# Four edits to the start of a three-layer kernel: more warming matmuls, two weight loads moved in the queue, two more large tiles, one split issued later

## The chip, the cores and the metric

The kernel runs on one core of a Trainium2 chip. The metric is the device time of one execution in microseconds. The kernel before has a median of 984.3 us over three runs (981.82 to 985.46). The execution that was profiled took 988.99 us; its span in the trace, from the first to the last instruction, is 987.2 us.

## The reference

The input x has 2 batches of 3008 rows of 256 numbers. Three layers follow one another:

```python
X = np.fft.fft(np.fft.fft(x, axis=1), axis=2).real        # (2, 3008, 256)
t = X.reshape(6016, 256)
h = t @ w_in;   t = (h / (1 + exp(-h))) @ w_out            # 256 -> 2048 -> 256
h = t @ w2_in;  t = (max(h, 0) + alpha * min(h, 0)) @ w2_out   # 256 -> 2048 -> 256
```

The weights arrive as 64-bit floats, so each one is converted to 32 bits on the chip.

## The kernel before, in words

**The transform** is a 64 by 47 factorisation of the 3008 rows, followed by the transform along the 256 columns. For each batch b it has three stages. Stage A (`stage_a`, L248) folds symmetric parts of x on DVE and POOL and multiplies by a 128x128 matrix that lies in `cs`; batch 0 uses the matrix as it is, batch 1 uses it split into a high and a low part, `fh` and `fl` (the split is a copy on ACT and a subtraction on DVE, L165 and L166). Its result `ya` goes to DRAM as `ys` and comes back transposed as `y`. Both ways are cut into three parts (`K_PARTS`): `store` (L295) writes part k, `load_y` (L312) reads it, with two stores and four loads for each part. Stage B (`stage_b`, matmul L325) multiplies y into `z`, in five groups for each half h; the first two groups need part 0 of y, the next two part 1, the last one part 2. Stage C (`stage_c`, matmul L355) makes `eo` and `n` from z, in three chunks of 502 columns for each batch.

**The first expert layer** has 96 iterations (six chunks of columns, 16 blocks of 128 of the 2048 hidden units). An iteration has six matmuls into `pe` and `po` (L560 to L562), three steps on DVE (`t`, `hp`, `t`: L568, L571, L572), Silu on ACT (`gh`, L575, and again L576), two subtractions `gl` (L588) on POOL or DVE, and twelve matmuls into accumulators (L608 to L612), two iterations later. The first 16 iterations run over blocks 0 to 7 of chunks 0 and 1. Weights come in four groups g of four blocks each: `load_w1(g)` issues two DMAs of 512 KB, `load_o1(g)` one of 1024 KB (both through `load_raw`, L393). A conversion is one ACT step (L181) and four DVE steps (L185 to L197) for each 512 columns; the high and low parts follow (L432, L435, L450, L454). Group 1 is used from iteration 4 on.

**The second expert layer** has the same sizes and runs afterwards, with its order written out by hand. Its coefficients come from `alpha` by six small POOL steps (`coefficients`, L483 to L488).

**What sets the order.** The start, up to stage C of the first chunk, stands in a `manual_schedule` block: each engine issues its instructions in the order of the text. All DMAs are issued by SP, one after another, and a DMA that waits holds up those behind it. Part 0 of y is stored and loaded first; 12 fp32 matmuls `warm` (L783, two records in the trace for each) follow stage A on PE. After stage C's first chunk the text stores part 1 of ys, loads part 1 of y, loads group 1's w_in, alpha, stores part 2, loads group 1's w_out and loads part 2 of y. Behind this block a planner, with its own costs of instructions, orders the rest up to the second expert layer. `put` gives each step the iteration in which it stands in the program's text (`PLAN`), and the planner may issue it earlier where an engine has nothing to do. `behind` forbids a step to be issued before a named instruction.

**Large tiles.** The pool `big` has 10 buffers of 8 KB in each partition. Pieces of x, raw weights, `ya`, `y`, `z` and `eo` take them in turn, so a load has to wait until the last user of its buffer is done.

Of the kernel before, what the change touches and what calls it, by code (L numbers as in the profile page):

```python
# [25 lines left out]
PLAN = {  # L26
# [5 lines left out]
}  # L32
# [15 lines left out]
F_PARTS = (0, 8, 16)  # L48
ORDER = [(c, f) for f0, f1 in zip(F_PARTS, F_PARTS[1:]) for c in range(2) for f in range(f0, f1)]
ORDER += [(c, f) for c in range(2, NC) for f in range(NF)]  # L50
WARM = 12
WARM0 = 8
SUM0 = "vpapap"
I1_AT = 0
# [11 lines left out]
FA0, FR0, R0, RS0, CD0, SD0, SG0, OD0, NCONST = 0, 128, 256, 444, 634, 762, 890, 1018, 1146  # L66
# [53 lines left out]
def fft_moe_kernel(  # L120
# [12 lines left out]
    nc = tc.nc  # L133
    wp = ctx.enter_context(tc.tile_pool(name="wp", bufs=1))
    dp = ctx.enter_context(tc.tile_pool(name="dp", bufs=1, space=bass.MemoryType.DRAM))
    bp = ctx.enter_context(tc.tile_pool(name="bp", bufs=10))
    ep = ctx.enter_context(tc.tile_pool(name="ep", bufs=3))
    cp = ctx.enter_context(tc.tile_pool(name="cp", bufs=5))
    kp = ctx.enter_context(tc.tile_pool(name="kp", bufs=16))
# [4 lines left out]
    def big(shape, dt, name):  # L144
        return bp.tile(shape, dt, tag="big", name=name)
# [4 lines left out]
    def conv(dt, name):  # L150
        return cp.tile([128, 512], dt, tag="cv", name=name)

    def mm_ps(name, w=512):
        return pm.tile([128, w], F32, tag="mm", name=name)
# [9 lines left out]
    def split(hi, lo, src, lo_eng=None):  # L164
        nc.scalar.activation(hi, src, AF.Copy)  # L165
        return (lo_eng or nc.vector).tensor_tensor(lo, src, hi.bitcast(F32), op=ALU.subtract)  # L166
# [57 lines left out]
    cs = wp.tile([128, CD0], F32, tag="cs", name="cs")  # L224
    fh = wp.tile([128, 128], F32R, name="fh")
    fl = wp.tile([128, 128], F32R, name="fl")
# [13 lines left out]
    def load_x(b, i, parts):  # L240
        n0, n1 = PIECES[i : i + 2]
        X[b, i] = t = big([128, 512 * (n1 - n0)], F32, f"x{b}_{i}")
        w = 512 * (n1 - n0) // parts
        for j in range(parts):
            at = 512 * n0 + j * w
            nc.sync.dma_start(t[:, j * w : (j + 1) * w], xs[b, :, at : at + w])
# [142 lines left out]
    def load_raw(key, *srcs):  # L389
        RAW[key] = t = big([128, 1024, 2], U32, f"raw_{key}")  # L390
        w = 2048 // len(srcs)
        for i, src in enumerate(srcs):
            nc.sync.dma_start(  # L393
                t.rearrange("p n t -> p (n t)")[:, i * w : i * w + w], src.bitcast(U32)
            )

    def load_half(key, src, i, at=None):
        if key not in RAW:
            RAW[key] = big([128, 1024, 2], U32, f"raw_{key}")
        at = i * 512 if at is None else at  # L400
        t = RAW[key].rearrange("p n t -> p (n t)")
        return nc.sync.dma_start(t[:, i * 1024 : i * 1024 + 1024], src[:, at : at + 512].bitcast(U32))
# [9 lines left out]
    def load_w1(g):  # L412
        load_raw(f"i{g}", wi1[0, :, 512 * g : 512 * g + 512], wi1[1, :, 512 * g : 512 * g + 512])

    def load_o1(g):
        load_raw(f"o{g}", wo1[:, 1024 * g : 1024 * g + 1024])

    def prep_w1(g):
        v = {}
        t = []  # L420

        def total(eng):
            wi_tiles(1, g)
            t.append(conv(F32, f"we{g}"))
            eng.tensor_tensor(t[0], v[0][0], v[1][0], op=ALU.add)

        def rest(eng):
            eng.tensor_tensor(v[0][0], v[0][0], v[1][0], op=ALU.subtract)
            t.append(v[0][0])

        def high(j):
            nc.scalar.activation(WI[1, g, 2 * j], t[j], AF.Copy)  # L432

        def low(j, eng):
            eng.tensor_tensor(WI[1, g, 2 * j + 1], t[j], WI[1, g, 2 * j].bitcast(F32), op=ALU.subtract)  # L435

        post = [either(total), either(rest)]
        for j in range(2):
            post += [lambda j=j: high(j), either(lambda eng, j=j: low(j, eng))]
        v[0], st0 = to_f32(None, (f"i{g}", 0, 512), f"i{g}_0")  # L440
        v[1], st1 = to_f32(None, (f"i{g}", 512, 512), f"i{g}_1")
        return [(st0, []), (st1, post)]
# [331 lines left out]
    def run(steps):  # L774
        for s in steps:
            (s if callable(s) else s[0])()

    def warm(w, x, n):
        if n == 0:
            return  # L780
        ps = mm_ps("warm")
        for j in range(n):
            nc.tensor.matmul(ps[:, : x.shape[1]], w, x, start=True, stop=True)  # L783

    if True:
        with tc.manual_schedule():
            zero = conv(F32, "zero")
            nc.vector.memset(zero[:, :256], 0.0)
            warm(zero[:, :128], zero[:, :256], WARM0)
            nc.vector.memset(sm, 0.0)  # L790
            nc.scalar.activation(sm[:1, :1], sm[:1, :1], AF.Silu)
            for j in range(len(PIECES) - 1):
                load_x(0, j, (PIECES[j + 1] - PIECES[j]) // 2)
                if j == 0:
                    nc.sync.dma_start(cs[:, :R0], cst[:, :R0])
            cc = conv(F32, "cc")
            for g in range(2):
                load_half("i0", wi1[g], g, 0)
                if g == 0:
                    nc.sync.dma_start(cc, cst[:, CD0:])  # L800
                    nc.sync.dma_start(w128_raw.rearrange("p n t -> p (n t)"), w128.bitcast(U32))
            nc.sync.dma_start(cs[:, R0:], cst[:, R0:CD0])
            fold, mm, rest = stage_a(0)
            (i00, _), (i01, after_i0) = prep_w1(0)
            for (h, i), n in zip(A_ORDER, A_WARM):
                if h == 0:
                    fold(i)
                mm(h, i)
                warm(cs[:, FA0 : FA0 + 128], cs[:, :256], n)
            load_half("o0", wo1, 0)  # L810
            for h in range(2):
                load_y(0, h, 0)
            load_half("o0", wo1, 1)
            warm(cs[:, FA0 : FA0 + 128], cs[:, :256], WARM)
            (s0, p0), (s1, p1) = prep_o1(0)
            w128_st = to_f32(lambda: w128_sb, ("w128", 0, NF), "w128")[1]
            run(i00[:4])
            run(i01[:2])
            run(w128_st[:1])
            nc.scalar.activation(ch, cc, AF.Copy)  # L820
            run(i00[4:])
            for ab in zip(i01[2:], w128_st[1:]):
                run(ab)
            run(w128_st[4:])
            nc.vector.tensor_tensor(cl, cc[:, : SG0 - CD0], ch.bitcast(F32)[:, : SG0 - CD0], op=ALU.subtract)
            for n, (st, pool) in enumerate(zip(after_i0, SUM0)):
                (st if callable(st) else st[pool == "v"])()
                if n == 2:
                    run(s0)
            b00, b01 = stage_b(0, 0), stage_b(0, 1)  # L830
            run(b00[:2])
            run(b01[:2])
            run(p0)
            run(s1[:EARLY_O0])
            run(stage_c(0, 0))
            rest(1)
            for h in range(2):
                load_y(0, h, 1)
            load_w1(1)
            nc.sync.dma_start(alpha_sb, alpha)  # L840
            rest(2)
            load_o1(1)
            for h in range(2):
                load_y(0, h, 2)
        n1 = NC * NF
# [9 lines left out]
        def put(a, b, steps):  # L855

            for j, st in enumerate(steps):
                plan.setdefault(a + (b - a) * j // len(steps), []).append(st)
# [5 lines left out]
        def behind(st, *at):  # L864
            with ExitStack() as stack:
                for k in at:
                    stack.enter_context(tc.issue_after(LAST[k].ins))
                run([st])
# [4 lines left out]
                nc.gpsimd.tensor_copy(cx[64 * j : 64 * j + 1, :], ch[:1, OD0 - CD0 : OD0 - CD0 + 128])  # L873

        put(*PLAN["cx"], [mixed_cosines])
        put(*PLAN["fa"], [lambda: split(fh, fl, cs[:, FA0 : FA0 + 128])])
        put(*PLAN["o0"], [lambda st=st: behind(st, 0, ("low", 0)) for st in s1[EARLY_O0:] + p1])
        put(*PLAN["i1"], [lambda st=st: behind(st, 0, ("t", I1_AT)) for st in staged(prep_w1(1))])
        put(*PLAN["o1"], staged(prep_o1(1)))
# [129 lines left out]
```

## Time and profile before

| | |
|---|---|
| median of three runs | 984.3 us |
| profiled execution / its span | 988.99 us / 987.2 us |
| PE busy | 957.9 us, 97% of the span |
| DVE busy | 780.8 us, 79% |
| ACT busy | 710.7 us, 72% |
| POOL busy | 405.4 us, 41% |
| data moved by DMA | 37.05 MB, all issued by SP |

A busy engine is one that executes an instruction. A start time in the trace is counted from the start of the span. In the rows "x14" means 14 instructions merged into one row, and what stands in brackets is the idle time of the engine before the row and what ended it. "PEclk" is the granted clock of TensorE, where 1.00 is 2.4 GHz and 0.50 is 1.2 GHz.

### The profile page before, as it was taken

What the parts mean: (1) busy time and instruction counts of PE and PEld (TensorE: products, weight loads), DVE (VectorE), ACT (ScalarE), POOL (GpSimd) and SP (SyncE); (2) the same over time, 40 slices, a digit from 0 to 9 for tenths busy, and PEclk for the clock granted to TensorE, in tenths of its full rate; (3) what the DMA queues carried; (4) which work ended last, traced back from release to release, by engine and by line L of the source; (5) the groups of instructions that cost most, each with busy time, mean ns of one, the idle gap of its engine ahead of it and who ended that gap; (6) DMA issues with size and microseconds to landing.
All of it is one profiled execution on the core that took longest, in us unless ns stands there. A gap on an engine that the chain in (4) does not pass through costs nothing.

```text
span 987.2 us, 14338 instructions
## 1 busy us (share of the span) xinstructions
PE 957.9 (97%) x5170; PEld 824.7 (84%) x5170; DVE 780.8 (79%) x1328; ACT 710.7 (72%) x1410; POOL 405.4 (41%) x355
## 2 busy tenths in 40 slices
PE   7889899999999999999899999999999999999998
PEld 5768787888878788787789999999999999999997
DVE  6888898676796876958687887878878788787876
ACT  3557566665667666666887888878888788787875
POOL 2677869333257467697641221312213122131200
PEclk9789999999999999999999999999999999999999
DMA  8730300230110201100000000000000000000000
GB/s 264 235 122 3 105 22 1 52 104 1 43 43 9 94 1 43 43 9 35 1 1 22 1 22 22 1 21 1 21 9 14 21 1 21 2 22 21 1 21 21
DMA packets 16614, 37.05 MB, mean 38 GB/s; under 512 B 1824, under 2 KB 11296, under 8 KB 14880
## 3 DMA queue, kind: packets, MB, share of 16 engines
q1 hardware_dynamic: 16544, 36.15, 11.1%
q8 instruction: 40, 0.66, 0.3%
q14 instruction: 30, 0.25, 0.1%
HBM read 26.83 MB, written 9.31 MB: 37 GB/s over the span
## 4 chain that ended last, share of the span: by engine, by line
PE 78%; DVE 9%; issue 5%; POOL 4%; ACT 3%; DMA 1%; SPq 0%; POOLq 0%; ACTq 0%; DVEq 0%
PE a L768 27%; PE ac L670 20%; PE a L610 5%; PE a L612 5%; PE a L608 5%; PE b L670 3%; POOL gl L588 2%; PE po L560 1%; PE po L561 1%; PE pe L560 1%; PE po L562 1%; DVE hp L571 1%; PE pe L562 1%; PE pe L561 1%; PE psb L325 1%
## 5 line engine op out<-in xcount | busy, mean ns | idle before, releaser
L768 PE MATMUL a<-gh,wo 128*128 128x502 f32 x768 | 268.2, 391 | 0.0
L588 POOL TENSOR_TENSOR gl<-t,gh 128x502 fp32r<-128x502 f32 x96 | 131.6, 1371 | 95.1 <-ACT t L576 81.6
L768 PEld LDWEIGHTS a<-gh,wo 128*128 128x128 f32 x768 | 145.0, 189 | 23.2
L737 DVE SCALAR_TENSOR_TENSOR h<-h,fc,q 128x502 f32<-128x502 f32 x192 | 130.3, 679 | 38.4 <-ACT q L732 35.7
L610 PE MATMUL a<-gl,wo 128*128 128x502 f32 x384 | 148.3, 395 | 4.1 <-POOL gl L588 4.1
L768 PE MATMUL a<-gl,wo 128*128 128x502 f32 x384 | 149.7, 391 | 0.0
L612 PE MATMUL a<-gh,wo 128*128 128x502 f32 x384 | 147.3, 393 | 0.0
L748 DVE TENSOR_TENSOR gl<-h,gh 128x502 fp32r<-128x502 f32 x192 | 140.5, 732 | 0.1
L575 ACT ACTIVATE gh<-hp 128x502 fp32r<-128x502 f32 x96 | 59.7, 622 | 92.6 <-DVE hp L571 90.6
L608 PE MATMUL a<-gh,wo 128*128 128x502 f32 x384 | 122.8, 397 | 1.2 <-ACT gh L575 0.8
L743 ACT ACTIVATE gh<-h 128x502 fp32r<-128x502 f32 x192 | 118.5, 617 | 2.1 <-DVE h L737 2.1
L732 ACT ACTIVATE q<-h,fc 128x502 f32<-128x502 f32 x192 | 116.9, 609 | 3.0 <-DVE h L715 1.5
L646 POOL TENSOR_TENSOR xt<-o 128x252 f32<-128x252 f32 x24 | 16.7, 716 | 187.2 <-ACT q L732 131.1
L568 DVE SCALAR_TENSOR_TENSOR t<-n,sm,pe 128x502 f32<-128x502 f32 x96 | 70.2, 731 | 29.0 <-PE pe L562 25.3
L610 PEld LDWEIGHTS a<-gl,wo 128*128 128x128 f32 x384 | 73.2, 191 | 20.7 <-POOL gl L588 5.9
L588 POOL TENSOR_TENSOR gl<-hp,gh 128x502 fp32r<-128x502 f32 x52 | 69.4, 1335 | 47.6 <-ACT hp L576 39.8
L571 DVE TENSOR_TENSOR hp<-t,po 128x502 f32<-128x502 f32 x96 | 64.5, 672 | 29.5 <-PE po L562 23.8
L608 PEld LDWEIGHTS a<-gh,wo 128*128 128x128 f32 x384 | 72.2, 191 | 17.5 <-ACT gh L575 2.2
L612 PEld LDWEIGHTS a<-gh,wo 128*128 128x128 f32 x384 | 73.1, 190 | 15.0
L768 PEld LDWEIGHTS a<-gl,wo 128*128 128x128 f32 x384 | 72.5, 189 | 7.7
L704 ACT ACTIVATE u<-ac 128x252 f32<-128x252 f32 x96 | 36.6, 381 | 51.6 <-PE ac L670 51.6
L656 POOL TENSOR_TENSOR os<-o,os 128x252 fp32r<-128x252 f32 x36 | 32.5, 918 | 94.5 <-ACT os L655 92.6
(191 smaller groups left out, 2296.0 us busy)
## 6 DMA issues: line engine op xcount, KB each, us to landing
out_t<-ot SPq DMA_DIRECT2D x24, 251.0 KB, 2.5
x<-in_xs SPq DMA_DIRECT2D x8, 512.0 KB, 5.6
raw_i<-in_wi SPq DMA_DIRECT2D x8, 512.0 KB, 4.7
raw_w<-in_wi SPq DMA_DIRECT2D x4, 1024.0 KB, 5.0
raw_w<-in_wo SPq DMA_DIRECT2D x4, 1024.0 KB, 4.8
raw_o<-in_wo SPq DMA_DIRECT2D x3, 1024.0 KB, 5.6
y<-ys SPq DMA_DIRECT2D x16, 144.0 KB, 2.9
x<-in_xs SPq DMA_DIRECT2D x2, 1024.0 KB, 4.8
```

Source lines behind the costliest of these rows:

```text
L568: nc.vector.scalar_tensor_tensor(t, E128[c], w128_sb[:, f : f + 1], pe, op0=ALU.mult, op1=ALU.add)
L571: nc.vector.tensor_tensor(hp, t, po, op=ALU.add)
L588: (nc.gpsimd if s or lo_pool(i + 1) else nc.vector).tensor_tensor(lo, h, hi.bitcast(F32), op=ALU.subtract)
L608: nc.tensor.matmul(ACC1[lb, s], hi, G[i, s][0], start=st, stop=False)
L610: nc.tensor.matmul(ACC1[lb, s], hi, G[i, s][1], start=False, stop=False)
L612: nc.tensor.matmul(ACC1[lb, s], lo, G[i, s][0], start=False, stop=sp)
L670: nc.tensor.matmul(to, w, x, start=start and q == 0, stop=q == 2, skip_group_check=True)
L732: nc.scalar.activation(h["q", i][:, to], source(n, part), AF.Abs, scale=coef(n, i, 1))
L737: nc.vector.scalar_tensor_tensor(h[f"h{i}"][:, to], source(n, part), coef(n, i, 0), h["q", i][:, to], op0=ALU.mult, op1=ALU.add)
L743: nc.scalar.activation(hi, H[n][f"h{i}"], AF.Copy)
L748: nc.vector.tensor_tensor(lo, H[n][f"h{i}"], G[n, i][0].bitcast(F32), op=ALU.subtract)
L768: nc.tensor.matmul(ACC2[lb], w[lb][j], x, start=st and first, stop=sp and last)
```

## The change

`WARM` goes from 12 to 20: eight more matmuls (16 records) behind stage A. `load_w1(1)` and `load_o1(1)` move ahead, from behind the loads of y's part 1 to the place right behind the second half of group 0's w_out; all three DMAs now stand ahead of the stores of ys parts 1 and 2. The pool of large tiles has 12 buffers, and the scratch for dynamic DMAs is set to 1024 bytes. The split of stage A's matrix for batch 1 is put `behind` the last instruction of stage C's first chunk.

```diff
-WARM = 12
+WARM = 20
...
-    bp = ctx.enter_context(tc.tile_pool(name="bp", bufs=10))
+    bp = ctx.enter_context(tc.tile_pool(name="bp", bufs=12))
...
             load_half("o0", wo1, 1)
+            load_w1(1)
+            load_o1(1)
             warm(cs[:, FA0 : FA0 + 128], cs[:, :256], WARM)
...
             for h in range(2):
                 load_y(0, h, 1)
-            load_w1(1)
             nc.sync.dma_start(alpha_sb, alpha)
             rest(2)
-            load_o1(1)
             for h in range(2):
                 load_y(0, h, 2)
...
-        put(*PLAN["fa"], [lambda: split(fh, fl, cs[:, FA0 : FA0 + 128])])
+        put(*PLAN["fa"], [lambda: behind(lambda: split(fh, fl, cs[:, FA0 : FA0 + 128]), 0)])
...
-    nc = _bacc.Bacc("TRN2", target_bir_lowering=False, num_devices=1)
+    nc = _bacc.Bacc("TRN2", target_bir_lowering=False, num_devices=1, dynamic_dma_scratch_size=1024)
```

## Rows read from the trace of the kernel before

**Rows 1.** The page's slices: granted clock in 40 slices of 24.7 us, in tenths.
```profile
PEclk9789999999999999999999999999999999999999
```

**Rows 2.** Stretches: start:end, length, busy us (count) by engine, clock, DMA share, GB/s.
```profile
8.60:16.20 7.60, 7.13 (x25) 4.17 (x25) 6.03 (x12) 3.73 (x8) 2.61 (x5) 1.00 0.91 351
16.20:21.60 5.40, 5.40 (x27) 4.43 (x25) 4.12 (x10) 2.30 (x6) 0.00 (x0) 1.00 0.76 165
21.60:25.00 3.40, 0.00 (x1) 0.03 (x1) 2.08 (x7) 1.79 (x3) 2.50 (x4) 0.97 0.83 250
25.00:35.00 10.00, 10.00 (x37) 8.80 (x38) 6.41 (x13) 4.03 (x11) 4.85 (x4) 0.50 0.74 219
35.00:57.00 22.00, 16.44 (x78) 12.53 (x77) 21.90 (x33) 13.41 (x27) 17.68 (x18) 0.97 0.67 226
57.00:62.00 5.00, 5.00 (x13) 3.96 (x13) 2.76 (x6) 2.97 (x5) 5.00 (x4) 0.50 0.25 101
```

**Rows 3.** Timeline of PE: start us, length us, engine, line, operation, tiles, shapes, count.
```profile
16.18 5.43 PE L783 MATMUL warm<-cs 128*128 128x256 f32 x24
25.00 3.27 PE L325 MATMUL psb<-cs,y 96*128 96x95 f32 x14 [3.40 <-DMA y<-ys]
28.45 2.45 PE L325 MATMUL psb<-cs,y 96*128 96x94 f32 x10
32.85 1.04 PE L355 MATMUL co<-z,ch 128*128 128x502 f32 x2
40.59 0.83 PE L325 MATMUL psb<-cs,y 96*128 96x94 f32 x6
43.66 0.49 PE L610 MATMUL a<-gl,wo 128*128 128x502 f32 x1 [2.24 <-POOL gl L588]
56.53 0.79 PE L560 MATMUL pe<-eo,wi 128*128 128x502 f32 x1 [2.02 <-DVE t L568]
63.15 0.62 PE L355 MATMUL co<-z,ch 128*128 128x502 f32 x2
```

**Rows 4.** Timeline of DVE and ACT from stage B to the first iteration.
```profile
25.89 1.64 DVE L197 SCALAR_TENSOR_TENSOR cvo<-raw_o,cvo 128x512 uint32<-128x512 uint32 x1
...
31.44 0.52 DVE L345 TENSOR_TENSOR z<-psb,z 128x219 fp32r<-128x219 f32 x2 [0.89 <-ACT z L343]
...
36.16 0.73 DVE L568 SCALAR_TENSOR_TENSOR t<-n,sm,pe 128x502 f32<-128x502 f32 x1
...
38.06 0.66 ACT L181 ACTIVATE cvi<-raw_i 128x512 f32<-128x512 f32 x1
```

**Rows 5.** Timeline of DVE in stage A of batch 0.
```profile
7.06 0.96 DVE L166 TENSOR_TENSOR fl<-cs,fh 128x128 fp32r<-128x128 f32 x1 [0.53 <-ACT fh L165]
...
9.91 0.69 DVE L258 TENSOR_TENSOR x<-x 128x512 f32<-128x512 f32 x1 [0.58 <-DMA x<-in_xs]
```

**Rows 6.** Timeline of SP's queue: issues of DMAs.
```profile
22.70 0.97 SPq L295 DMA_DIRECT2D ys<-ya  x2
29.11 2.60 SPq L312 DMA_DIRECT2D y<-ys  x4
31.82 0.83 SPq L393 DMA_DIRECT2D raw_i<-in_wi  x2
32.70 0.43 SPq L840 DMA_DIRECT2D sm<-in_alpha  x1
```

**Rows 7.** DMA issues up to 60 us: count, KB each, median us to landing.
```profile
raw_i<-in_wi SPq DMA_DIRECT2D x8, 512.0 KB, 4.7
...
y<-ys SPq DMA_DIRECT2D x8, 144.0 KB, 3.3
...
sm<-in_alpha SPq DMA_DIRECT2D x1, 8.0 KB, 6.0
```

**Rows 8.** Timeline of POOL: the first coefficient step and the first `gl`.
```profile
39.49 0.38 POOL L483 TENSOR_SCALAR fc<-sm 128x16 f32<-128x16 f32 x1
...
41.91 1.69 POOL L588 TENSOR_TENSOR gl<-hp,gh 128x502 fp32r<-128x502 f32 x1
```

## The prediction

> **What bounds the kernel now.** I read the page's slices first. PE's clock is at its full level almost throughout, and the second slice is the one that shows a clear loss [rows 1]. So I cut the first 62 us into stretches [rows 2]. In them the reader sees four things. From 16.2 to 21.6 PE is busy without a gap at clock 1.00, with warming matmuls that end at 16.18 + 5.43 = 21.61 [rows 3]. From 21.6 to 25.0 PE does nothing, and in the next 10 us its granted clock is 0.50, that is 1.2 GHz. From 35 to 57 DVE is busy for 21.90 of 22.00 us, so there DVE sets the pace, with POOL at 17.68 behind it. From 57 to 62 PE is busy without a gap, again at 0.50. Behind that PE is the bound for the rest of the kernel (97% of the span), which no edit touches directly. The timeline of PE says what ended the first idle time: y's arrival, at 25.00 after 3.40 us [rows 3].
>
> So the change can win time in two places: in the 10 us at half clock, and in what follows from an earlier start of the stretch that DVE bounds. In 25 to 35 DVE has 10.00 - 6.41 = 3.59 us without work [rows 2]. What is won can't be more than that until DVE itself gets less to do.
>
> **Warming matmuls.** 24 records take 5.43 us, 0.226 us each [rows 3]; 16 more take 3.62 us. PE is then busy until 21.61 + 3.62 = 25.23. Y is there at 25.00, so stage B starts 0.23 us later than before. In return the clock should still be at 1.00 there, since PE has no idle time before it. Stage B's records at 1.2 GHz: 14 in 3.27 us and 10 in 2.45 us, 0.24 us each. At 2.4 GHz: 6 in 0.83 us, 0.138 us each [rows 3]. For 24 records that is 5.7 us against 3.3 us. With the two small matmuls in between (0.25 us) stage B ends at 25.23 + 3.3 + 0.25 = 28.8 instead of 28.45 + 2.45 = 30.90, so 2.1 us earlier.
>
> What is late next is DVE. Its low parts of z come in four steps behind the conversion step that ends at 25.89 + 1.64 = 27.53 [rows 4]; that conversion doesn't depend on PE and stays where it is. With two steps of about 0.45 and two of about 0.52 us they can't end before 29.4. Counted from PE's end instead, they end as before 1.06 us behind it (31.96 against 30.90), at 29.9. I take the middle, 29.6, which is 2.35 us earlier than 31.96. Stage C and the first iteration follow: a pair of stage C's matmuls took 1.04 us at half clock and 0.62 us at full clock [rows 3], 0.2 us for each of the four that lie between the last z and the second output, 0.8 us. DVE works beside them and takes 4.2 us from its last z to the first `t` (31.96 to 36.16, rows 4), of which it waits about 0.9 us. I let 0.5 us of that go. Together the first `t` starts 2.85 us earlier, with 0.2 us lost as the lower end (clock at half in spite of the matmuls: only the 0.23 us of overhang stay) and 3.59 us as the upper end (all of DVE's idle time filled).
>
> Beside this the Trainium skill, "TensorE: Matmul & The Clock Gate", section "What's actually happening", says that the clock is held at half by default, that activity releases it, and that the moment of a change varies from run to run, because the window that the chip looks at isn't tied to the kernel. The profiled execution agrees with the first two (0.97 in the idle stretch, 0.50 behind it); one execution can't show the third. By the third the fall to 0.50 need not be in each run; that is the second rival below.
>
> **Group 1's loads ahead of y's later parts.** SP issues three more DMAs, 2 x 512 KB + 1024 KB = 2.1 MB, before the two stores of ys part 1 that it issued at 22.70 [rows 6]. The issue itself costs 0.83 us for two and about 0.4 to 0.7 for the third. The transfer costs more: at the 351 GB/s of the busiest stretch 2.1 MB take 6.0 us, at the 250 GB/s of the stretch before 25.0 8.4 us [rows 2]. Part 0 of y is issued earlier and isn't behind them. The stores of part 1 land that much later, so the loads of y's part 1, at 29.11 before, go out at 35.1 to 37.5, and with 0.8 us for the first two and 3.3 us to landing [rows 6, 7] the half that is used first is there at 39.2 to 41.6. PE reads it at 40.59 before, and would do so at 37.7 now. It may wait 1.5 to 3.9 us there. Right behind this on PE's queue stands a matmul that waited 2.24 us for POOL anyway [rows 3]; it covers the wait that I take (1.5, nearest to the rate of the stretch with full queues), and leaves 1.7 at the far end. Two more groups on the same part come later. I cost this at 0, with 0 to 1.7 us of loss.
>
> What the move saves: raw_i of group 1 was issued from 31.82 to 32.65 and landed 4.7 us after issue, about 37.3 [rows 6, 7]; ACT read it at 38.06 [rows 4]. With everything else 2.85 us earlier ACT would come at 35.2 and wait 2.1 us, and DVE, the bound, behind it. Now it is issued at about 23.7 and lands, with raw_o behind it, within 6.0 us, before 31. So the move wins nothing against before, but without it most of the gain would be lost.
>
> Alpha, the stores of part 2 and the loads of part 2 stay behind y's part 1 on SP and go 6.0 us later with it. Part 2 is used much later (stage C's third chunk). Alpha is a rival below.
>
> **Twelve large tiles.** Without them the moved loads would have to wait for buffers; with 11 tiles taken up to raw_o of group 1 they don't. Later loads may be issued earlier; none of PE's waits of this stretch was for one. I cost it at 0, from -1 to +1 us, about what a new order by the planner may move in the waits of 2 us that the rows show. The smaller scratch I cost at 0: all data goes out by SP's own queue, and nothing in the rows uses another.
>
> **The split.** `fl` took DVE 0.96 us at 7.06, ahead of the folds [rows 5]. Taking it out wins nothing there: DVE's next fold but one waits for x's DMA until 9.91. It comes back behind stage C's first chunk, in or after the stretch where DVE has 0.10 us free [rows 2]. There it costs from 0 (put into a later gap) to 0.96 us. I take 0.4, since half as many columns as a 512-column step that takes 0.7 us without contention would be below that, and POOL is busy beside it.
>
> **The sum.** 2.85 - 0.4 = 2.45 us less, so 986.5 us for the profiled execution of 988.99 (span 987.2 and 1.8 around it). That execution is 4.7 us above the median of the three runs; I take the difference from the median: 984.3 - 2.4 = 981.9 us. Its own range is 980.3 to 983.5.
>
> **Rivals.**
>
> *More than the start is won.* The half-clock stretch from 57 to 62 has 13 matmuls at 0.42 instead of 0.23 us, 2.5 us. It follows a wait of 2.02 us for DVE at 56.53 [rows 3]. If POOL's coefficient steps, which hold it from 39.49 to 41.91 ahead of the first `gl` [rows 8], land elsewhere in the new order, POOL slows DVE less, that wait shrinks and the clock stays up. Then 2.4 + 2.5 = 4.9 us are won, up to 6.1 with all of DVE's idle time: 979.4 to 978.2. For it: the planner makes its order anew. Against it: DVE has as much to do as before.
>
> *The fall of the clock is not in every run.* The three runs lie 3.6 us apart, the profiled one 3.5 us above the slowest. If the median run has no half-clock stretch at 25 us, the warming matmuls remove nothing there, and the change is worth +0.2 (overhang) + 0.4 (split) - 0.5 (order of the loads): 984.4. For it: the runs' distance is about the size of the gain. Against it: the idle time of 3.4 us is set by DMA, the same in each run.
>
> *Slower: POOL waits for alpha.* In the trace the coefficient steps stand on POOL ahead of the first `gl`, 39.49 and 41.91 [rows 8]. Alpha was issued 3.6 us behind the first load of y's part 1 (0.8 us of it for raw_i) [rows 6]; at 35.1 + 2.8 = 37.9 now, landing after 3.3 (like y) to 6.0 us [rows 7], at 41.2 to 43.9. If the planner again puts the coefficients ahead of the first `gl`, POOL stands until then, and with the 2.42 us that they take the first `gl` starts at 43.6 to 46.3, 1.7 to 4.4 us later than before. PE waits for it and everything behind shifts: 986.0 to 988.7, say 987.4. It decides if alpha lands later than 39.5 and the order on POOL stays. For it: SP's order puts alpha behind everything that is delayed. Against it: the coefficients were put there only because POOL had nothing else; now the `gl` would be ready before.
>
> **How the numbers follow.** Forecast 48%, more won 23%, no fall in the usual run 15%, POOL waits 14%. A measurement of this kernel can tell a difference of about 0.5%, 4.9 us, from none. Faster than 979.4 takes most of the first rival and the forecast's tail, 25%. Slower than 989.2 takes the upper half of the last, with losses at y's part 1 added, 7%. The rest, 68%, is within. The range 977.5 to 986.8 leaves out the lower end of the first rival and the upper half of the last.
>
> **What would show it.** Right: no idle time of PE between 21.6 and 25, clock near 1.00 from 25 on, the first `t` at 33 to 34, raw_i of group 1 landed before ACT reads it. Wrong: a clock of 0.50 behind the longer warming; PE waiting at 38 for y's part 1 by more than 2.2 us; coefficient steps ahead of the first `gl` with POOL idle before them; DVE idle between 33 and 54; the first stretch that PE fills less than 2 us earlier than 57.

## The result and the profile after

The changed kernel is slower: a median of 989.75 us over four runs (988.78 to 991.53) against 983.62 us for the kernel before in the same session (981.82 to 985.46). The ratio is 1.0064, 95% interval [1.0039, 1.0089], that is 6.3 us more (3.8 to 8.8). 2.4 us less were forecast. The profiled execution took 988.78 us, its span is 987.0 us. That is no longer than the profiled span before (987.2): the profiled execution of before was 4.7 us above its median, as the table said, and this one is 1 us below its own. So the totals of these two traces don't show the loss; they are compared stage by stage, and all totals below are ratios of many runs to the kernel before on the same chip; us are worked out as (ratio - 1) x 984.8, the median before in most sessions.

The stretches after, in the columns of [rows 2]; the fourth and fifth were not cut before:

```profile
25.00:35.00 10.00, 8.73 (x47) 6.56 (x45) 8.58 (x16) 6.98 (x17) 4.07 (x3) 1.00 0.83 283
35.00:57.00 22.00, 12.46 (x46) 9.50 (x47) 15.12 (x28) 8.01 (x16) 14.28 (x15) 0.77 0.68 230
57.00:62.00 5.00, 4.50 (x24) 3.34 (x23) 2.95 (x7) 4.94 (x12) 5.00 (x5) 1.00 0.26 108
42.70:53.00 10.30, 6.67 (x21) 5.49 (x22) 3.46 (x5) 3.09 (x6) 6.73 (x9) 0.50 0.75 298
25.00:62.00 37.00, 25.69 (x114) 19.40 (x113) 26.66 (x49) 19.93 (x43) 23.36 (x22) 0.86 0.66 228
```

The first row holds the gain: the clock is 1.00 where it was 0.50. The second holds the loss: DVE, which was busy for 21.90 of 22.00 us there, has work for 15.12, and PE for 12.46. From 25 to 62 PE stands for 37.00 - 25.69 = 11.3 us; before it was 37.00 - (10.00 + 16.44 + 5.00) = 5.6 us.

A second profile of the kernel before (984.5 us, first under "The experiments") is nearer to its median, and against it the loss stands in the first 65 us. The fifth `hp` on DVE, that of iteration 4, in the whole change and in that second profile:

```profile
65.05 0.68 DVE L571 TENSOR_TENSOR hp<-t,po 128x502 f32<-128x502 f32 x1 [3.18 <-PE po L562]
...
59.34 0.68 DVE L571 TENSOR_TENSOR hp<-t,po 128x502 f32<-128x502 f32 x1 [0.32 <-PE po L562]
```

That is 5.7 us; at the end these two spans differ by 4.3 us (987.0 and 982.7). In the first profile of before the same step starts at 62.02.

PE after, for [rows 3]:

```profile
15.27 8.88 PE L783 MATMUL warm<-cs 128*128 128x256 f32 x40
24.27 1.77 PE L325 MATMUL psb<-cs,y 96*128 96x95 f32 x14
...
26.14 1.35 PE L325 MATMUL psb<-cs,y 96*128 96x94 f32 x10
...
37.55 0.84 PE L608 MATMUL a<-gh,wo 128*128 128x502 f32 x3
46.33 0.79 PE L610 MATMUL a<-gl,wo 128*128 128x502 f32 x1 [7.93 <-POOL gl L588]
...
48.17 1.43 PE L325 MATMUL psb<-cs,y 96*128 96x94 f32 x6
```

The warming matmuls reach y, and stage B's first 14 records take 1.77 us instead of 3.27. Then, at 38.4, PE stands for 7.93 us for a `gl`; before, the same wait was 2.24 us. Stage B's third group, `psb` from y's part 1, stands *behind* that wait; before it stood ahead of it, at 40.59. What held the `gl` is told by the chain of work that ended last, cut to 30 to 56 us (start, length, what):

```profile
23.44 10.76 DMA ys<-ya
...
36.09 2.97 DMA sm<-in_alpha
...
39.14 1.76 POOL fc L483
...
41.32 3.03 POOL wo L454
...
45.08 1.21 POOL gl L588
...
46.33 0.79 PE a L610
...
48.37 1.24 PE psb L325 x6
...
49.63 0.41 ACT z L343
```

It is to be read downwards: the stores of ys part 1, issued at 23.44 behind the moved loads, take 10.76 us. SP waits for them to load y's part 1, and alpha stands behind that. POOL needs alpha for the coefficients, has them ahead of the first `gl`, with one step of 3.03 us (`wo`, L454) among them, and PE waits for the `gl`. SP's own rows, for [rows 6]:

```profile
21.82 0.91 SPq L393 DMA_DIRECT2D raw_i<-in_wi  x2
22.77 0.54 SPq L393 DMA_DIRECT2D raw_o<-in_wo  x1
23.44 1.76 SPq L295 DMA_DIRECT2D ys<-ya  x2
34.34 1.71 SPq L312 DMA_DIRECT2D y<-ys  x4
36.09 0.42 SPq L841 DMA_DIRECT2D sm<-in_alpha  x1
```

and POOL's, for [rows 8]:

```profile
28.60 1.30 POOL L454 TENSOR_TENSOR wo<-cvo,wo 128x512 fp32r<-128x512 f32 x1 [0.82 <-ACT wo L450]
39.14 1.76 POOL L483 TENSOR_SCALAR fc<-sm 128x16 f32<-128x16 f32 x1 [9.25 <-DMA sm<-in_alpha]
...
41.29 3.06 POOL L454 TENSOR_TENSOR wo<-cvo,wo 128x512 fp32r<-128x512 f32 x1
...
45.03 1.24 POOL L588 TENSOR_TENSOR gl<-hp,gh 128x502 fp32r<-128x502 f32 x1
```

DVE after, from the first iteration on, for [rows 4]:

```profile
32.33 0.73 DVE L568 SCALAR_TENSOR_TENSOR t<-n,sm,pe 128x502 f32<-128x502 f32 x1
...
34.23 0.43 DVE L185 TENSOR_SCALAR cvo<-cvo 128x512 f32<-128x512 f32 x1 [0.57 <-ACT cvo L181]
34.58 0.67 DVE L571 TENSOR_TENSOR hp<-t,po 128x502 f32<-128x502 f32 x1
...
35.50 0.29 DVE L166 TENSOR_TENSOR fl<-cs,fh 128x128 fp32r<-128x128 f32 x1
35.70 0.42 DVE L189 TENSOR_SCALAR cvo<-cvo 128x512 uint32<-128x512 uint32 x1
36.04 0.67 DVE L572 TENSOR_TENSOR t<-t,po 128x502 f32<-128x502 f32 x1
...
40.76 0.67 DVE L571 TENSOR_TENSOR hp<-t,po 128x502 f32<-128x502 f32 x1
...
50.07 0.45 DVE L345 TENSOR_TENSOR z<-psb,z 128x282 fp32r<-128x282 f32 x1 [6.84 <-ACT z L343]
```

Group 1's w_out is on the chip earlier, so the planner issues its conversion steps (`cvo`) among the steps of the first two iterations. And DVE stands for 6.84 us at 43.2, because its next step needs the `psb` that PE has behind the waiting matmul.

### The profile page after: what moved, and what is told of

Same layout as the page of the kernel before. It is cut to its first block, busy times and chain, and to the rows that moved or that the text cites. A ratio compares the mean times of both kernels' runs of the same rounds, so it can differ in the third digit from the quotient of the medians.

```text
span 987.0 us, 14377 instructions
## 1 busy us (share of the span) xinstructions
PE 957.1 (97%) x5186; PEld 822.9 (83%) x5186; DVE 775.7 (79%) x1328; ACT 710.4 (72%) x1410; POOL 405.3 (41%) x355
## 4 chain that ended last, share of the span: by engine, by line
PE 82%; DVE 6%; POOL 3%; issue 3%; DMA 3%; ACT 2%; SPq 0%; DVEq 0%; POOLq 0%; ACTq 0%
PE a L768 27%; PE ac L670 20%; PE a L610 7%; PE a L608 6%; PE a L612 6%; PE b L670 3%; PE pe L560 2%; PE pe L562 2%; PE po L560 2%; PE pe L561 2%; PE po L562 2%; PE po L561 2%; DMA ys<-ya 2%; PE psa L281 1%; POOL gl L588 1%
## 5 line engine op out<-in xcount | busy, mean ns | idle before, releaser
L588 POOL TENSOR_TENSOR gl<-t,gh 128x502 fp32r<-128x502 f32 x96 | 129.6, 1350 | 91.9 <-ACT t L576 65.4
```

Of the source, the lines that this page charges most:

```text
L588: (nc.gpsimd if s or lo_pool(i + 1) else nc.vector).tensor_tensor(lo, h, hi.bitcast(F32), op=ALU.subtract)
```

## The experiments

Fifteen kernels ran, in four sessions. The first theory was that the move loses the time through alpha: POOL stands for it ahead of the first `gl`. The rivals were the edits themselves (the split, the tiles, the longer warming), the later landing of y's part 1, and, once the order on DVE was seen, w_out's conversions ahead of `t`. This table takes the edits one by one; the interval is 95%.

| kernel | ratio to before | us |
|---|---|---|
| whole change | 1.0064 [1.0039, 1.0089] | +6.3 |
| longer warming alone | 0.9979 [0.9968, 0.9990] | -2.1 |
| split alone | 1.0010 [1.0000, 1.0020] | +1.0 |
| twelve tiles and scratch alone | 0.9998 [0.9987, 1.0009] | -0.2 |
| moved loads alone | 1.0048 [1.0032, 1.0064] | +4.7 |
| whole change, move undone | 0.9992 [0.9983, 1.0001] | -0.8 |

**The kernel before, again** (no edit).

> The kernel before, unchanged, for a second profile: the profiled execution of before took 988.99 us, its other runs 981.82 to 985.46. Theory 'clock': the 5 us are the two half-clock stretches (25 to 35 and 57 to 62 us), and a usual run lacks one or both: if this profile's time is near 984, its granted clock is near 1.00 in at least one of the two. Rival 'spread': the 5 us are spread over the whole span, and both stretches are at 0.50 again with a time near 984.

One execution: 984.5 us, span 982.7. Two of its stretches, as in [rows 2]:

```profile
25.00:35.00 10.00, 10.00 (x38) 8.72 (x38) 6.43 (x13) 4.60 (x11) 4.15 (x3) 0.55 0.70 209
...
57.00:62.00 5.00, 4.83 (x21) 3.69 (x20) 4.20 (x9) 4.36 (x9) 5.00 (x5) 1.00 0.13 52
```

The fall of the clock behind the wait for y is there again; the one at 57 us isn't. A shorter one stands at 44.5 to 47.4 us instead, by matmuls of 0.62 us where the others take 0.39. Not every fall in one trace belongs to the kernel.

**The coefficients later.** The whole change, and:

```diff
+ put(*PLAN["co"], [lambda: behind(coefficients, ("gl", 8, 1))])
```

> The changed kernel, with the six coefficient steps on POOL held behind the gl of iteration 8; no DMA moves. Theory 'POOL waits for alpha' (9.25 us idle on POOL, PE waits 7.93 us for the first gl): the wait goes, the first gl starts at 37 to 39 us instead of 45.0, and PE's first matmul on it at 38 to 40 instead of 46.3; 6 to 8 us less, 982 to 984 us. Rival 'y part 1 is late': PE waits for it instead (it is loaded from 34.3 on), stage B's next group stays at 46 to 48 us and the time at 988 or more. Rival 'the planner's order lost the time elsewhere': under 2 us less.

1.0017 [1.0002, 1.0032], +1.7 us. POOL's first `gl` starts at 35.72. 4.6 us of the loss go, less than the 6 to 8 expected; that they go with the wait for alpha is the theory, since this edit also makes a new order (its own price is asked below).

**Alpha first.** The whole change, with alpha's DMA ahead of group 1's loads:

```diff
+            nc.sync.dma_start(alpha_sb, alpha)
             load_w1(1)
             load_o1(1)
...
-            nc.sync.dma_start(alpha_sb, alpha)
```

> The changed kernel, with alpha's DMA issued right ahead of the second groups' raw weights instead of behind y's part 1. Theory 'POOL waits for alpha': POOL's idle 9.25 us go, coefficients run at 24 to 30 us, the first gl at 37 to 39, and the time is 982 to 985 us. Rival 'y part 1 is late': still 988 or more, with PE waiting for y. Rival 'planner's order': under 2 us less.

1.0011 [0.9996, 1.0026], +1.1 us. Again most of the loss is gone, with 8 KB moved. The wait for alpha isn't gone but moved: POOL now stands 2.67 us for it at 27.33, ahead of the low parts of group 0's w_in (L435). The order of the conversions on DVE stays. In DVE's timeline of this run the second `t` of the first iteration is later than in the whole change (36.04):

```profile
37.99 0.67 DVE L572 TENSOR_TENSOR t<-t,po 128x502 f32<-128x502 f32 x1
```

and in PE's timeline PE waits for it:

```profile
38.71 0.79 PE L560 MATMUL po<-eo,wi 128*128 128x502 f32 x1 [2.44 <-DVE t L572]
```

**The move undone.** The whole change, with the three loads back:

```diff
-            load_w1(1)
-            load_o1(1)
...
+            load_w1(1)
             nc.sync.dma_start(alpha_sb, alpha)
             rest(2)
+            load_o1(1)
```

> The changed kernel with the loads of the second groups' raw weights back at their old places (20 warming matmuls, 12 tiles and the later split stay). Theory 'POOL waits for alpha': alpha is issued about 32 us again and the first gl starts at 39 to 42; the warming matmuls' gain stays in part; ACT waits some 2 to 5 us for raw_i of group 1: 982 to 985 us. Rival 'the moved loads are innocent, the loss is in the planner's order or in the tiles': 988 or more.

0.9992 [0.9983, 1.0001]. The move costs 6.3 + 0.8 = 7.1 us on top of the other edits. That places the loss; the next runs ask for its parts.

**The longer warming alone.** The kernel before, and:

```diff
-WARM = 12
+WARM = 20
```

> The kernel before with 20 warming matmuls and nothing else. Theory 'the gain at the start is lost again where DVE and POOL set the pace' (in the changed kernel with the loads moved back, the first pe starts at 30.2 instead of 34.1 us and 20 us of PE's work are done at 52.0 against 52.1): first pe at 30 to 31, ACT waits for raw_i of group 1, a half-clock stretch at about 40 in place of that at 25, 20 us of work done at 51 to 53, total within 1.5 us of before. Rival, the forecast: 2.4 us less than before.

0.9979 [0.9968, 0.9990]: 2.1 us faster, better than both kernels and the lowest ratio of all runs (0.9981 below can't be told from it). The theory, that the gain is lost again further on, fails; the forecast of 2.4 us is what came. Its trace shows a small form of the same wait, in POOL's timeline:

```profile
38.08 0.20 POOL L483 TENSOR_SCALAR fc<-sm 128x16 f32<-128x16 f32 x1 [1.75 <-DMA sm<-in_alpha]
```

in PE's timeline, where `psb` stands ahead of the wait:

```profile
38.56 0.80 PE L325 MATMUL psb<-cs,y 96*128 96x94 f32 x6
41.27 0.79 PE L610 MATMUL a<-gl,wo 128*128 128x502 f32 x1 [1.91 <-POOL gl L588]
```

and in the stretch from 25 to 62, in the columns of the stretches:

```profile
25.00:62.00 37.00, 31.31 (x143) 24.62 (x144) 33.73 (x54) 23.47 (x48) 28.59 (x26) 0.91 0.63 204
```

PE stands for 5.7 us from 25 to 62, 5.6 less than in the whole change. The two kernels lie 8.4 us apart, these two spans 5.4.

**The moved loads alone.** The kernel before with 12 warming matmuls and 10 tiles, the split as before:

```diff
             load_half("o0", wo1, 1)
+            load_w1(1)
+            load_o1(1)
...
-            load_w1(1)
...
-            load_o1(1)
```

> The kernel before (12 warming matmuls, 10 tiles, the split as it was) with the second groups' raw weights loaded ahead of y's later parts. Theory 'the moved loads delay alpha, and POOL waits for it ahead of the first gl': POOL idle until 38 to 40 us with the coefficients first, the first gl at 43 to 46 us (41.9 before), PE waits 3 to 6 us for it; 987 to 990 us. Rival 'it needs the earlier start by the warming matmuls': first gl before 43, within 1.5 us of before.

1.0048 [1.0032, 1.0064], +4.7 us. In POOL's timeline it stands for alpha, as in the whole change:

```profile
38.81 0.40 POOL L483 TENSOR_SCALAR fc<-sm 128x16 f32<-128x16 f32 x1 [6.05 <-DMA sm<-in_alpha]
```

and in PE's timeline PE stands for the `gl`, with `psb` behind it at 46.10:

```profile
44.32 0.73 PE L610 MATMUL a<-gl,wo 128*128 128x502 f32 x1 [3.80 <-POOL gl L588]
```

So the larger part of the loss needs neither the other edits nor an earlier start. But it isn't made up here as in the whole change. In POOL's and DVE's timelines:

```profile
42.59 1.68 POOL L588 TENSOR_TENSOR gl<-hp,gh 128x502 fp32r<-128x502 f32 x1
...
41.42 3.39 DVE L193 SCALAR_TENSOR_TENSOR cvo<-raw_o,cvo 128x512 uint32<-128x512 uint32 x2
44.74 0.66 DVE L571 TENSOR_TENSOR hp<-t,po 128x502 f32<-128x502 f32 x1
```

The `gl` starts only 0.7 us later than before (41.91), and DVE waits 0.31 us for its `z` at 48.01, not 6.84. Iteration 1's `hp` stands behind w_out's conversion steps and starts 2.3 us later than before (42.42).

**The coefficients later and w_out held.** The run "coefficients later", and:

```diff
-        put(*PLAN["o1"], staged(prep_o1(1)))
+        put(*PLAN["o1"], [lambda st=st: behind(st, ("t", 1)) for st in staged(prep_o1(1))])
```

> The changed kernel with the coefficients behind the gl of iteration 8 and the conversion of group 1's w_out on DVE held behind the t of iteration 1. With the coefficients alone held back it took 986.4 us. Theory 'what is left of the loss is that w_out's conversion, possible early now, stands on DVE ahead of the first t': the first t (L572) at about 35 instead of 38 us, 2 to 3 us less, 983 to 984.5 us. Rival 'what is left is y part 1, 9 us later': the first group of stage B on it still waits beyond 42 us, 986 or more.

0.9996 [0.9987, 1.0006]: 2.1 us better than the coefficients later alone; the two intervals just touch.

**The loads behind the stores.** The run "coefficients later", with w_in of group 1 behind the stores of ys part 1 and w_out of group 1 behind those of part 2, its place in the kernel before:

```diff
-            load_w1(1)
-            load_o1(1)
...
             rest(1)
+            load_w1(1)
             for h in range(2):
                 load_y(0, h, 1)
             nc.sync.dma_start(alpha_sb, alpha)
             rest(2)
+            load_o1(1)
```

> The changed kernel with the raw weights loaded in another order: w_in of group 1 behind the stores of y part 1 and ahead of its loads, w_out of group 1 behind the stores of part 2; coefficients behind the gl of iteration 8. Theory: raw_i lands at about 31 to 33, y part 1 no more than 2 us later than before, no coefficient ahead of the first gl: no wait for DMA on ACT, POOL or PE between 25 and 45 us, first gl at 37 to 39; 981 to 983 us, under both kernels. Rival 'DVE and POOL have the same work to do up to 57 us and hold it': within 1 us of the kernel with the loads moved back, 983.8.

0.9981 [0.9969, 0.9992]. The run stands where the longer warming alone stands, though PE doesn't wait for `gl` at all. Against the longer warming with the coefficients later (0.9998, below), which shares that edit, it is 1.7 us better, so what this smaller move is worth isn't settled. DVE sets the pace again, as the busy time of its stretch shows:

```profile
35.00:57.00 22.00, 18.00 (x72) 13.22 (x73) 21.52 (x33) 13.14 (x27) 17.23 (x14) 0.84 0.71 255
```

**The split alone.** The kernel before, and:

```diff
+ put(*PLAN["fa"], [lambda: behind(lambda: split(fh, fl, cs[:, FA0 : FA0 + 128]), 0)])
```

> The kernel before with the split of stage A's matrix issued later, and nothing else. Forecast: 0 to +0.96 us, taken as +0.4. Theory from the profiles so far (fl on DVE takes 0.28 to 0.30 us without contention, beside the first t, and its place at 7 us delays the first fold): within 0.5 us of before, so no difference that can be told. Rival: stage A ends about 0.9 us earlier, as it does in the changed kernel's profile (warming starts at 15.27 instead of 16.18), and 0.5 to 1 us are won.

1.0010 [1.0000, 1.0020], +1.0 us, above the 0.5 us expected; the rival's gain of 0.5 to 1 us doesn't come. `fl` itself takes 0.28 us at 37.3, in the stretch in which DVE sets the pace, and its copy on ACT stands beside it.

**Twelve tiles and the scratch alone.**

```diff
-bufs=10
+bufs=12
...
+ dynamic_dma_scratch_size=1024
```

> The kernel before with 12 large tiles and the smaller scratch, and nothing else. Forecast: 0, from -1 to +1 us. Theory: SP's order is the same and none of PE's waits is for a large tile, so within 1 us of before. Rival 'the planner's new order of the middle part costs what is left of the loss': 1.5 to 2.5 us more than before.

0.9998 [0.9987, 1.0009]: nothing.

**The moved loads alone, coefficients later.** "Moved loads alone" with the edit of "coefficients later".

> The kernel before with the moved loads and the coefficients behind the gl of iteration 8 (12 warming matmuls, 10 tiles). The moved loads alone took 4.7 us more than before. Theory 'POOL waits for alpha is the larger part': 2.5 to 4 us of these go, 986 to 988 us, no idle time on POOL that alpha ends; what stays (1 to 2 us) is w_out's conversion ahead of the first t on DVE and y's part 1. Rival 'another effect of the moved loads': less than 1.5 us go.

1.0032 [1.0019, 1.0044]: only 1.6 us better than the move alone, where 2.5 to 4 were expected. Either the wait for alpha is a small part, or holding the coefficients back has a price; the next run asks that.

**The longer warming alone, coefficients later.** "Longer warming alone" with the same edit.

> 20 warming matmuls and the coefficients behind the gl of iteration 8; loads, tiles and split as before. The warming alone took 2.1 us less than before and POOL waited 1.75 us for alpha in its profile. Theory: that wait goes and the first gl starts at 37 to 38.5 instead of 40.0; 0.5 to 1.5 us less than the warming alone, about 982. Rival 'DVE sets the pace there, not POOL': the same time as the warming alone, within 0.5 us.

0.9998 [0.9989, 1.0006], against both the theory and its rival. Holding the coefficients back costs 1.9 us by itself here, so it is no clean way to take the wait for alpha away. By the two traces, one execution each, the time goes by the clock, not by a wait: from 25 to 62 us PE stands for 5.1 us here and 5.7 in the longer warming alone, at a mean clock of 0.82 and 0.91. The longer warming alone has one half-clock stretch there (matmuls of 0.62 us from 41.85 to 46.5, 0.39 outside). This run has a short one (six `psb` take 1.43 us at 38.64, against 0.80) and a long one:

```profile
50.50:60.70 10.20, 9.56 (x26) 6.95 (x25) 8.23 (x13) 5.62 (x11) 10.20 (x8) 0.50 0.32 105
```

Open behind these twelve was how the loss divides between POOL's wait for alpha and the conversions ahead of `t`. Three more runs asked for it.

**w_out held, nothing else.** The whole change, with the edit to `PLAN["o1"]` shown above; alpha stays late, and the coefficients stay ahead of the first `gl`.

> The whole change, with one edit: the steps of group 1's w_out conversion may not be issued before the t of iteration 1. The coefficients stay on POOL ahead of the first gl and alpha stays late. Theory of two parts (POOL's wait for alpha costs 3 to 4 us, the conversion steps ahead of t on DVE some 2 us): 987.5, ratio 1.0025 to 1.004 against before, with POOL still idle over 6 us for alpha. Rival (the wait for alpha is the whole loss, the order of the conversions costs nothing while POOL stands): like the whole change, 1.0064, 991 us.

1.0016 [1.0006, 1.0026], +1.6 us, 4.7 us better than the whole change. POOL still stands for alpha almost as long, by its timeline:

```profile
38.89 0.73 POOL L483 TENSOR_SCALAR fc<-sm 128x16 f32<-128x16 f32 x1 [8.88 <-DMA sm<-in_alpha]
...
41.70 1.30 POOL L588 TENSOR_TENSOR gl<-hp,gh 128x502 fp32r<-128x502 f32 x1
```

PE's timeline has a much shorter wait, with `psb` ahead of it:

```profile
37.53 0.88 PE L325 MATMUL psb<-cs,y 96*128 96x94 f32 x6
43.05 0.79 PE L610 MATMUL a<-gl,wo 128*128 128x502 f32 x1 [4.64 <-POOL gl L588]
```

and DVE's timeline has the step that needs this `psb`:

```profile
39.48 0.44 DVE L345 TENSOR_TENSOR z<-psb,z 128x282 fp32r<-128x282 f32 x1
...
49.37 0.52 DVE L345 TENSOR_TENSOR z<-psb,z 128x157 fp32r<-128x157 f32 x2 [2.63 <-ACT z L343]
```

DVE has its `z` at 39.48 instead of 50.07, works through the wait, and its longest idle time is 2.63 us instead of 6.84. This edit does more than that, though: the first `gl` starts at 41.70 instead of 45.03, no later than before (41.91), with L454 at 1.26 us instead of 3.06 and two of the six coefficient steps behind it. So part of the 4.7 us can be the earlier `gl` itself.

**Alpha first and w_out held.** The whole change with both edits.

> The whole change with both edits: alpha's DMA ahead of group 1's loads, and the w_out steps of group 1 behind the t of iteration 1. Theory of two parts: both losses gone, 0.9975 to 0.999, 982.5 to 983.5 us, like the warming alone with the split's cost. Rival (a third cost of the move, such as y's part 1 coming later or more DMA beside the work, is as large as these two): 1.001 or more, 985 us or more, with PE waiting for y.

1.0009 [0.9999, 1.0018], +0.9 us: hardly better than either alone. With the twelve above:

| | w_out free | w_out held |
|---|---|---|
| coefficients ahead of `gl`, alpha late | +6.3 | +1.6 |
| coefficients ahead of `gl`, alpha first | +1.1 | +0.9 |
| coefficients later | +1.7 | -0.4 |

The two causes don't add up. In the first two rows, with the other taken away, w_out's conversions cost 0.2 us and alpha's wait 0.7; together they cost 5.4, so 4.5 us come from both at once, give or take 3 by the four intervals. The first and the last row give 2.6, which these intervals don't tell from nothing. The theory of two parts, 3 to 4 and some 2 us, which the expectations held, doesn't fit: with w_out held 1.6 us are left where 2.5 to 3.9 were expected, and with both taken away the time is 0.9 us over before, where 1.0 to 2.5 less were expected. The rival that POOL's wait is the whole loss falls. The rival of a third cost had 1.001 or more, with PE waiting for y: the time fits, but PE waits 0.2 us for y in this trace.

**The longer warming alone, alpha first.**

```diff
             load_half("o0", wo1, 1)
+            nc.sync.dma_start(alpha_sb, alpha)
...
-            nc.sync.dma_start(alpha_sb, alpha)
```

> The kernel before with the longer warming alone, and with alpha's DMA (8 KB) issued right behind the first half and the second half of group 0's w_out, ahead of y's later parts. In the run with warming alone POOL stood 1.75 us for alpha, and PE 1.9 us for the first gl. Theory (POOL's wait for alpha costs PE about what POOL stands): 1 to 2 us better than the warming alone, ratio 0.996 to 0.997, 981 to 982 us. Rival (DVE sets the pace of 35 to 57 us, a gl that comes earlier changes nothing): like the warming alone, 0.998, 983 us.

1.0008 [0.9999, 1.0017]: 2.9 us *worse* than the longer warming alone, against both theories. With alpha there early the planner puts the first coefficient steps ahead of the low parts of group 0's w_in (L435), and POOL stands for alpha there:

```profile
28.13 0.20 POOL L483 TENSOR_SCALAR fc<-sm 128x16 f32<-128x16 f32 x1 [3.15 <-DMA sm<-in_alpha]
```

So this edit moves the wait and doesn't remove it: the low parts start at 28.46 instead of 24.78, POOL's first `gl` 0.67 us earlier only (39.30 against 39.97), and a half-clock stretch reaches into 57 to 62 (0.76 there, 1.00 in the longer warming alone). What of the 2.9 us is which isn't settled. POOL stands in the same place in both runs of the whole change with alpha first (2.67 and 3.31 us). So the two edits that take away the wait ahead of the `gl` have prices of their own, 1.9 and 2.9 us on the longer warming alone. The whole change with both causes taken away lies 0.7 and 2.0 us above warming and split together (-1.1); these prices can hold that rest, and no third cost of the move is needed for it, though none is excluded.

## Why the prediction was wrong

**Warming: right.** 2.85 us at the first `t` were forecast, 2.4 with the split's 0.4 off; the edit alone brought 2.1 [1.0 to 3.2]. The steps came as written: no idle time of PE until y, clock 1.00 behind it, stage B in 1.77 + 1.35 us and what lies between, the first `t` at 32.33 (33.3 forecast, y being there 0.7 us earlier in this execution). Group 1's raw weights need not come earlier for it: the prediction held that without the move "most of the gain would be lost", and the longer warming alone keeps 2.1 us, though ACT waits 1.05 us for raw_i in it.

**Twelve tiles: right,** 0 forecast, -0.2 measured. **The split** was taken at 0.4 with 0.96 as its end, and cost 1.0 [0 to 2.0]; the 128 columns of `fl` are a quarter of a 512-column step, not half, and alone it took 0.28 us at its new place, so its length wasn't what the later split costs. The sum's own range, 980.3 to 983.5, is narrower than its terms: their ends add up to 979.7 to 988.2, and the measured loss lies beyond even that.

**The moved loads: the step that failed.** They were costed at 0 to 1.7 us and cost 4.7 alone and 7.1 on top of the rest. Three points of its working:

First, y's part 1. The stores were to land so that y goes out at 35.1 to 37.5; it went out at 34.34, 0.8 us ahead of that, and no wait of PE for y's part 1 is in the trace. This part held. Raw_o was to land before 31, the 2.1 MB being put at 6.0 us; ACT waited 1.67 us for it until 33.53, 11.7 us after the first of the loads was issued, and DVE stood 0.57 us behind that. What this cost no run shows.

Second, alpha. "Alpha is a rival below": that rival came, with 14% given to it. Its first `gl` was to start at 43.6 to 46.3 and did at 45.03, by luck: alpha landed at 39.06, not at 41.2 to 43.9, and the coefficients, with L454 among them, held POOL for 5.9 us, not 2.42. The reason given against it, that the `gl` would now be ready before and so stand first, was a guess about the planner, and wrong: the order on an engine is fixed before anything runs, by the planner's own times, and all six coefficient steps stand ahead of the `gl` both in the whole change and with alpha first.

Third, the price. The rival's 987.4 took the delay of the first `gl` against before (1.7 to 4.4 us) as the whole loss, 3.1 us; the `gl` did come 3.1 us later than before, and 6.3 were measured. What it left out is that the moved weights also change DVE's and PE's order. With w_out's conversions ahead, iteration 1's `hp` starts at 40.76 instead of 37.68 (w_out held), the planner puts `psb` behind the matmul that waits for `gl`, and the wait for alpha then stops not only that matmul but, through `psb` and `z`, DVE. None of the rivals had this. The prediction said "everything behind shifts" without asking what stands behind. Shown: with w_out held `psb` is ahead again and 4.7 us go, though POOL stands as long; with alpha first `psb` stays behind (43.06) but nothing waits there, and 5.2 us go. In the five traces with all three loads moved and w_out's conversions free, `psb` stands behind the first matmul on a `gl`; in the other twelve it stands ahead. Argued only: that the place of `psb` is the whole of the coupling. No run moved `psb` alone, and holding w_out also brought the `gl` 3.3 us forward. Open: what the 4.7 us of the moved loads alone are made of, where the `gl` is hardly late and DVE doesn't stand for `psb`; no run held w_out there.

**The clock.** The rival that the fall isn't in every run was half true. The fall behind the wait for y came in both traces of the kernel before (0.50 and 0.55), so the warming has something to remove; the fall at 57 us came in one of the two (0.50 and 1.00), while the other has a shorter one at 44.5 to 47.4 us. The Trainium skill, "TensorE: Matmul & The Clock Gate", section "What's actually happening", says that the moment of a change varies from run to run; by these two traces it does. The rival "more than the start is won" counted 2.5 us on that second fall, which an equal execution doesn't have there. In the whole change the clock adds to the loss: at 46.33, behind 7.93 us without work, PE starts at half clock and keeps it until 53 (0.50 in the stretch 42.70 to 53.00 above).

## What to carry to other kernels

A load moved ahead delays every DMA behind it in the queue, also an 8 KB one, and the price is read by asking which engine has the user of that small load in front of work that is ready. Ask then what stands behind the waiting instruction on the next engine: POOL's wait for alpha cost 0.7 us with w_out's conversions held, where PE fed DVE first, and 5.2 with them free, where it didn't. Moving the small load ahead moves the wait: with alpha first POOL stood 2.7 to 3.3 us for it further ahead. Where a planner fixes the order, an earlier arrival is an edit of every engine's order; time such an edit alone before it is joined to others, and compare medians, since one profiled execution here lay 4.7 us off.

## What the runs showed of the hardware

- Two stores of ys took 10.76 us behind 2.1 MB of loads on the same queue. In the trace before they had been issued at 22.70, and SP could load what they wrote at 29.11, 6.4 us later [rows 6].
- 512-column steps of POOL and DVE take longer in some stretches where both work, now on the one side, now on the other: POOL's L454 took 1.30 us at 28.60 and 3.06 at 41.29 in the whole change, beside DVE's conversion steps of 0.69 us; in the moved loads alone two of DVE's L193 took 3.39 us from 41.42 on, beside POOL's steps of 1.44 and 1.68 us.
- The clock also falls without a long wait ahead: in the longer warming with coefficients later it is 0.50 from 50.50 to 60.70, and PE's longest idle time between 35 and 50.5 was 1.28 us.
